# Fixed SBUF homes, a tile of its own for the first relu, and weight chunks fetched two ahead, in a fused attention, mixing and gating kernel

## The chip, the cores and the metric

The kernel runs on one core of a Trainium2 chip. The metric is the device time of one execution in microseconds (us); lower is better. A core has a matrix engine (TensorE, PE in the rows, its weight loads PEld), a vector engine (VectorE, DVE), a scalar engine (ScalarE, ACT), GpSimd (POOL) and SyncE (SP), whose queue issues the transfers of this kernel. Operands lie in SBUF, 128 partitions wide; products are collected in eight PSUM banks.

## The reference

Batch 8, 8 heads, sequence 576, head width 64, 32 memory slots; model width 512, inner width 1024.

```python
a = softmax(phi, axis=seq)                       # over the 576 positions
k_m, v_m = a^T k, a^T v                          # 32 slots per head
x = softmax(q k_m^T / 8) v_m                     # heads side by side: 576 x 512
x_prev = x shifted by one position, zero first
xk = mu_k * x + (1 - mu_k) * x_prev ;  xr likewise with mu_r
x2 = sigmoid(xr @ w_r) * (relu(xk @ w_k)**2 @ w_v)
h = relu(x2 @ w_in) ;  u, v = halves of h
v_n = (v - mean) / sqrt(var + 1e-6)
out = (u * (w_spatial @ v_n + b_spatial)) @ w_out
```

The weights arrive as 64-bit floats.

## The kernel before, in words

**Products.** To keep precision, every operand is split into a high and a low part by `split` (L124 to L128: a copy on ScalarE, a subtraction on VectorE), and a product is three matmuls: high by high, low by high, high by low. `gemm` (L102) issues them, so nearly all matmuls of the kernel have line 106; those of the wide value product have line 847. Each matmul has its own weight load of 128 columns. The moving operand has 288 columns (early and in the spatial product), 504 (the wide blocks), 256 or 512 (the last two products).

**Stages.** (1) Two attention steps and the first mixing, at 0 to about 150 us; `k_phase`, `r_phase` and `v_product` work on 288 columns twice, i = 0 and 1. (2) Eight wide blocks j = 0 to 7 of 504 columns, to about 616 us: in each, eight products K, eight V and four R in the order K0 K1 K2 V0 K3 V1 ... V5 R0 R1 R2 V6 R3 V7. K ends in a relu, a square and a split (L829, L830, `split`) into one of three slots of the tiles kh and kl, which V reads; R ends in a sigmoid (L837) out of bank 4 or 5 into tile r. (3) The products with w_in (seven products in place of eight, on 256 columns, `uv`), layer norm and the spatial product (`spatial`, 288 columns), to about 920 us. (4) The product with w_out (`project`).

**What runs between the products.** `pump()` is called 40 times in a wide block, in the middle of a product and behind it. Each call advances `att`, the generator of the attention steps 2 to 15 (`att_step`, 19 steps each), by `pace[1]`, 0.95, steps, and the generator `more[0]` by one. The end of an attention step splits its probabilities into the tile asp (ScalarE L382, VectorE L383) and, one step on, multiplies them on TensorE. The attention of block j + 2 waits until block j has made its xr. In block 6, behind K3, `more[0]` becomes `w_in_steps()`, which turns the chunks of w_in, and then of w_out, from 64-bit into 32-bit floats and forms their combinations and splits.

**Weight conversion.** `load_f64` (L155 to L180) first issues the transfer of a chunk into one of the buffers st0 and st1 (L151, SyncE's queue), and right behind it the conversion: L163 on ScalarE, L171 and L173 on VectorE. Each engine takes its instructions in order. The order itself is not quite that of the program: a planner that knows the dependences and estimates durations places an instruction earlier where it sees its operands ready; `tc.issue_after` (the `behind` of L137) forbids it to place an instruction ahead of a named one.

**Where buffers lie.** Every name has one place in SBUF; places are given out in the order in which names are first claimed, each rounded up to 32 bytes. A new tile of a name waits for the accesses to the old one. From sizes and order, the starts modulo 128 bytes are, before: kh, asp, r, t2, xs1 to xs7, AT, W1, W2, W3, st0, st1, xT1 at 0; kl, xT0, xs0, t1 at 32; t0 at 64. Inside a tile of 504 columns the low part begins 2016 bytes behind the high part, which is 96 modulo 128.

Of the kernel before, what the change touches and what calls it, by code (L numbers as in the profile page):

```python
# [38 lines left out]
WIDTHS = [1024, 1024, 1024, 1024, 512]  # L39


PARTS_K = [(0, 1, "st0"), (1, 1, "st1"), (2, 2, "xT1"), (4, 2, "kl"), (6, 1, "st0"), (7, 1, "st1")]
# [6 lines left out]
def kernel(  # L49
# [31 lines left out]
    def turns(*tags):  # L81

        while True:
            yield from tags

    ident_sb = tile_of("ident", [128, 128])
# [163 lines left out]
    def att_step(i):  # L250
# [83 lines left out]
        for halves in ((0,), (1,)) if i < 2 else ((0, 1),):  # L334
# [43 lines left out]
            else:  # L378
                for pr in range(2):
# [61 lines left out]
    def prep_x(which, c, p0, p1, both=None):  # L441
# [18 lines left out]
        if both is None:  # L460
            both = operand(n)
        h, lo = both[:, 0:p1 - p0], both[:, p1 - p0:2 * (p1 - p0)]
        split(x32, h, lo)
# [9 lines left out]
            tile_of("ATh", [128, 4096]), q0, rest[:, 0:2 * S], rest[:, 2 * S:2 * S + 256],  # L473
            rest[:, 2 * S + 256:], tile_of("asp", [128, 1792], F32R),
        ),
# [85 lines left out]
    def w_in_steps():  # L561
# [22 lines left out]
        while not att_free:  # L584
            yield
        room = tile_of("asp", [128, 1792])
        parts_of("AT", wi_v)
        for j in range(2):
            at = []
            for half in range(2):  # L590
                at.append(load_f64(part(1, half, j)))
                yield
            (a11, a12), (a21, a22) = ((v[:, 0:2], v[:, 2:4]) for v in at)
            h, lo = (p[:, :, :, 128 * j:128 * j + 128] for p in wi_v)
            raw = room[:, 0:768].rearrange("p (q c f) -> p q c f", q=3, c=2)
            add(raw[:, 0], a21, a22, ALU.add)
            add(raw[:, 1], raw[:, 0], a11)
            add(raw[:, 2], a11, a21)
            for q, a in ((0, a11), (1, a12), (2, a22), (3, raw[:, 0]), (4, raw[:, 1]), (5, raw[:, 2])):
                split(a, h[:, q], lo[:, q])  # L600
                if q % 2:
                    yield
            add(raw[:, 0], a12, raw[:, 1])
            split(raw[:, 0], h[:, 6], lo[:, 6])
            yield
        a11, a12, a21, a22 = (quads[:, half, 2 * k:2 * k + 2] for half in range(2) for k in range(2))
        s1, s2, s4 = (room[:, 512 * n:512 * n + 512].rearrange("p (c f) -> p c f", c=2) for n in range(3))
# [10 lines left out]
        for f0 in range(0, DM, 128):  # L618
            load_f64(chunks[:, :, 2 * f0:2 * f0 + 256], raw=wo_raw[:, :, f0:f0 + 128])
            yield  # L620
        for k in range(2):
# [12 lines left out]
    x2s = {}  # L634
    w1_free, xT_free, att_free = [], [], []
    copied, added, left_v, normal = [None], [None], [], []
# [83 lines left out]
    def k_phase(i, after):  # L720
        xk = [xs[0, c] for c in range(KC)]
        kh, kl = pair("k", [128, FC, HB])
        room = tile_of("r", [128, 6, HB])
        r, ks = room[:, 0:KC], room[:, KC:]
        for m in range(FC):
# [5 lines left out]
            ))  # L731
            nc.scalar.activation(out=ks[:, m % 2, :], in_=acc, func=ACTF.Relu)
            if m % 2 == 1:
                two = slice(m - 1, m + 1)
                x = ks
                nc.scalar.activation(out=x, in_=x, func=ACTF.Square)
                copied[0] = split(x, kh[:, two, :], kl[:, two, :])
# [82 lines left out]
    for j in range(NB):  # L820
        p0 = S + WB * j
        p1 = p0 + WB
        v_accs = []

# [34 lines left out]
        for n, (f, c) in enumerate(order):  # L859
            f(c)  # L860
            if f is K and c < KC:
                prep_x(1, c, p0, p1, last_xr if c == KC - 1 else None)
                if c == KC - 1:
                    mixed.add(j)
                    if j == NB - 2:
                        for _ in att:
                            pass
                        att_free.append(True)
                        more[0] = w_in_steps()
                    elif j == NB - 1:  # L870
# [344 lines left out]

    for tag, n in (("asp", 6), ("t2", 1), ("r", 7), ("xs7", 2)):
        big = tile_of(tag, [128, n * HB], F32R)
# [145 lines left out]
```

## Time and profile before

| | us |
|---|---|
| median of 3 runs | 1010.55 (1009.86 to 1014.23) |
| the profiled execution's own time | 1009.7 |
| its span | 1007.9 |
| TensorE busy | 977.4 (97%) |
| VectorE busy | 692.2 |
| ScalarE busy | 616.8 |
| GpSimd busy | 94.1 |

Matmuls overlap in TensorE's pipeline: a matmul of 504 columns is listed with about 0.39 us, but starts follow each other every 0.23 us. So a busy TensorE is not an unhindered one, and the pace is read from the distance of starts.

### The profile page before, as it was taken

The page shows a single profiled execution, that of the slowest core. Times are in us where ns is not written, and L with a number is a line of the kernel's source. Part 1 is how long each engine was busy: PE and PEld are TensorE (multiplying, and loading weights), DVE is VectorE, ACT ScalarE, POOL GpSimd, SP SyncE. Part 2 cuts the span into 40 slices and gives each one's busy share as a digit, 9 for nine tenths or more (in the row PEclk, how much of TensorE's full clock was granted, in tenths as well). Part 3 has the DMA queues.
Part 4 walks back from the last instruction along what each step waited for, and adds up shares of the span by engine and source line. Part 5 has one row for each costly group of instructions (what it writes and reads, how often), then busy time and mean ns, then how long its engine had stood idle before and what let it go on. Part 6 is the DMA issues. An engine that isn't in the chain of part 4 may idle for free.

```text
span 1007.9 us, 16735 instructions
## 1 busy us (share of the span) xinstructions
PE 977.4 (97%) x6404; PEld 855.3 (85%) x6404; DVE 692.2 (69%) x1409; ACT 616.8 (61%) x1177; POOL 94.1 (9%) x70
## 2 busy tenths in 40 slices
PE   5879999999999999999998999999999999999998
PEld 4678878787777787777887889999999999998887
DVE  4988785736757467574666417868777767869983
ACT  3786975757757577575666545936544644564653
POOL 0000000000000000000013002022012402203320
PEclk8989999999999999999999999999999999999999
DMA  9486351421334223340041502231142223155643
GB/s 279 143 259 188 114 152 64 143 79 45 122 102 143 78 56 112 102 131 1 1 154 54 169 11 84 78 113 33 58 131 86 79 78 89 56 180 162 209 147 115
DMA packets 85008, 110.93 MB, mean 110 GB/s; under 512 B 18112, under 2 KB 68416, under 8 KB 82624
## 3 DMA queue, kind: packets, MB, share of 16 engines
q1 hardware_dynamic: 84928, 109.87, 34.5%
q8 instruction: 50, 0.82, 0.3%
q14 instruction: 30, 0.25, 0.1%
HBM read 79.43 MB, written 30.41 MB: 109 GB/s over the span
## 4 chain that ended last, share of the span: by engine, by line
PE 73%; DVE 11%; ACT 11%; DMA 3%; issue 1%; POOL 1%; SPq 0%; DVEq 0%; ACTq 0%; POOLq 0%
PE bank L106 58%; PE bank L847 13%; DVE t L454 2%; DVE xs L126 1%; PE bank L289 1%; ACT t L451 1%; DMA st<-in_w_in 1%; DMA ATh<-in_kv 1%; DVE kh L126 1%; DVE r L882 1%; DVE kl L126 1%; ACT t L830 1%; ACT t L829 1%; ACT xs L125 1%; ACT L362 1%
## 5 line engine op out<-in xcount | busy, mean ns | idle before, releaser
L106 PE MATMUL bank<-xs,W1h 128*128 128x504 f32 (+2 forms) x1112 | 240.8, 335 | 0.3 <-ACT xT L943 0.3
L106 PEld LDWEIGHTS bank<-xs,W1h 128*128 128x128 f32 x1112 | 182.0, 190 | 23.2 <-issue 3.1
L847 PE MATMUL bank<-kh,W3h 128*128 128x504 f32 x384 | 129.1, 393 | 0.0
L106 PE MATMUL bank<-xs,W1l 128*128 128x504 f32 (+2 forms) x556 | 128.3, 335 | 0.0
L106 PEld LDWEIGHTS bank<-xs,W1l 128*128 128x128 f32 x556 | 94.1, 190 | 10.5 <-issue 0.2
L847 PEld LDWEIGHTS bank<-kh,W3h 128*128 128x128 f32 x384 | 72.2, 188 | 17.9 <-issue 2.8
L106 PE MATMUL bank<-xs,W2h 128*128 128x504 f32 (+3 forms) x316 | 79.8, 371 | 2.9 <-ACT r L837 2.5
L454 DVE SCALAR_TENSOR_TENSOR t<-xT,mu,t 128x288 f32<-128x288 f32 (+6 forms) x128 | 63.0, 512 | 27.1 <-ACT t L451 26.6
L106 PE MATMUL bank<-ATh,xs 128*128 128x256 f32 x472 | 75.3, 281 | 0.0
L847 PE MATMUL bank<-kh,W3l 128*128 128x504 f32 x192 | 75.1, 391 | 0.0
L829 ACT ACTIVATE t<-bank 128x504 f32<-128x504 f32 x64 | 37.5, 586 | 60.2 <-PE bank L106 52.0
L451 ACT ACTIVATE t<-xT,mu 128x288 f32<-128x288 f32 (+6 forms) x128 | 65.0, 532 | 15.0 <-DVE xs L126 14.3
L126 DVE TENSOR_TENSOR kh<-t,kh 128x504 fp32r<-128x504 f32 x48 | 33.2, 692 | 49.4 <-ACT kh L125 49.2
L106 PEld LDWEIGHTS bank<-xs,W2h 128*128 128x128 f32 x316 | 54.7, 188 | 13.6 <-ACT r L837 3.0
L106 PEld LDWEIGHTS bank<-ATh,xs 128*128 128x128 f32 x472 | 64.4, 188 | 0.1
L126 DVE TENSOR_TENSOR xs<-st,xs 128x512 fp32r<-128x512 f32 (+1 forms) x60 | 52.8, 891 | 13.7 <-ACT xs L125 13.7
L126 DVE TENSOR_TENSOR xs<-t,xs 128x504 fp32r<-128x504 f32 (+1 forms) x72 | 44.4, 624 | 24.3 <-ACT xs L125 24.0
L125 ACT ACTIVATE xs<-st 128x512 fp32r<-128x512 f32 (+1 forms) x60 | 36.1, 624 | 38.4 <-POOL st L662 35.4
L125 ACT ACTIVATE xs<-t 128x504 fp32r<-128x504 f32 (+1 forms) x72 | 39.6, 577 | 26.4 <-PE bank L106 16.2
L662 POOL TENSOR_TENSOR st<-st 128x512 f32<-128x512 f32 x16 | 23.7, 1481 | 257.3 <-DVE xs L126 256.7
L106 PE MATMUL bank<-ATl,xs 128*128 128x256 f32 x236 | 47.2, 282 | 0.0
L391 POOL MEMSET xT<- 128x4 f32 x8 | 0.9, 107 | 445.0 <-DVE t L454 366.4
(283 smaller groups left out, 2159.2 us busy)
## 6 DMA issues: line engine op xcount, KB each, us to landing
ATh<-in_kv SPq DMA_DIRECT2D x14, 1300.0 KB, 6.3
ATl<-in_qT SPq DMA_DIRECT2D x30, 288.0 KB, 4.3
st<-x2d SPq DMA_DIRECT2D x32, 256.0 KB, 3.9
ATh<-in_phin SPq DMA_DIRECT2D x15, 320.0 KB, 2.9
st<-in_w_in SPq DMA_DIRECT2D x8, 512.0 KB, 4.0
ATh<-gd SPq DMA_DIRECT2D x8, 512.0 KB, 4.9
out_T<-W3h SPq DMA_DIRECT2D x16, 256.0 KB, 2.7
out_T<-W3l SPq DMA_DIRECT2D x16, 256.0 KB, 2.6
```

The costliest lines, as they stand in the source:

```text
L106: x = nc.tensor.matmul(out=out, lhsT=pairs[i][0], rhs=pairs[i][1], start=fresh and i == 0, stop=i == n - 1, skip_group_check=not fresh,)
L125: high = nc.scalar.activation(out=h, in_=x, func=ACTF.Copy)
L126: low = nc.vector.tensor_tensor(out=lo, in0=x, in1=h.bitcast(F32), op=ALU.subtract)
L289: x = nc.tensor.matmul(out=kvp[32 * j:32 * j + 32, :], lhsT=ph[0:n, t, 32 * j:32 * j + 32], rhs=kv[0:n, t, j, :], start=(t == 0), stop=(t ...
L362: nc.scalar.activation(out=st[:, bl], in_=st[:, bl], func=ACTF.Exp, scale=scale)
L451: nc.scalar.activation(out=x, in_=xT[b][:, c, s0:s0 + w], func=ACTF.Copy, scale=mu_sb[:, 2 * KC + n:2 * KC + n + 1])
L454: nc.vector.scalar_tensor_tensor(out=x, in0=xT[b][:, c, 1 + s0:1 + s0 + w], scalar=mu_sb[:, n:n + 1], in1=x, op0=ALU.mult, op1=ALU.add,)
L662: engine.tensor_tensor(out=out, in0=a, in1=b, op=ALU.subtract)
L829: nc.scalar.activation(out=x, in_=acc, func=ACTF.Relu)
L830: nc.scalar.activation(out=x, in_=x, func=ACTF.Square)
L847: nc.tensor.matmul(out=v_accs[m], lhsT=a, rhs=b, start=c == 0 and n == 0, stop=c == FC - 1 and n == 2,)
L882: added[0] = nc.vector.tensor_tensor(out=x2, in0=v_accs[m], in1=x2, op=ALU.mult)
```

## The change

Three parts. **Homes:** all names are claimed at the start in a written order and size (`HOMES`), with a gap of 64 bytes ahead of the weights. Modulo 128, kh, kl, asp, r, t2 and xs0 to xs7 then start at 0, and W1, W2, W3, AT, st0, st1 and xT1 at 64 (xT0 at 96); the low part of a 504-column operand begins 2048 bytes behind the high part. asp becomes smaller, t2 larger. **Relu:** in `k_phase` the result of the relu goes to a new tile of t2 for each pair of m, no longer to the end of tile r. **Conversions:** `conversions()` fetches two chunks ahead of the one that it converts, with two steps on either side of each conversion; conversions and splits are placed behind the last K or R copy (`copied[0]`); `w_in_steps` starts at the head of block 6 and not behind K3, takes the AT part first and the part in xT0 second; block 7 advances it six more times. Beside these, an attention step has one more empty step between splitting its probabilities and multiplying them (20 in all), and `pace[1]` is 1.0.

```diff
+HOMES = [
+    ("ident", 512), ("mask", 32), ("mu", 64), ("eps", 32),
+    ("kh", 9216), ("kl", 9216), ("asp", 6656), ("r", 8064), ("t2", 2304),
+    ("xs0", 4096), ...
+    ("xs7", 2304), ("gap", 64),
+    ("W1h", 16384), ("W1l", 16384), ("W2h", 8192), ("W2l", 8192), ("W3h", 16384), ("W3l", 16384),
+    ("ATl", 16384), ("ATh", 16384), ("st0", 4096), ("st1", 4096), ("xT1", 9248), ("xT0", 9248),
+    ("t0", 2016), ("t1", 2016),
+]
+    for tag, n in HOMES:
+        tile_of(tag, [128, n // 4])
...
             yield True
+            if not wide:
+                yield False
...
-        h, lo = both[:, 0:p1 - p0], both[:, p1 - p0:2 * (p1 - p0)]
+        low = HB if n == 7 and p1 - p0 == HB else 512
+        h, lo = both[:, 0:p1 - p0], both[:, low:low + p1 - p0]
...
-        quads = tile_of("xT0", [128, 2, KC, HALF])
-        for half in range(2):
-            for j in range(2):
-                load_f64(part(0, half, j), raw=quads[:, half, :, 128 * j:128 * j + 128])
-                yield
-                yield
+        def conversions(todo):
+            bufs = [fetch(src) for src, _ in todo[:2]]
+            for n, (src, raw) in enumerate(todo):
+                for _ in range(2):
+                    yield
+                with behind(copied[0]):
+                    load_f64(bufs[n], raw=raw)
+                for _ in range(2):
+                    yield
+                if n + 2 < len(todo):
+                    bufs.append(fetch(todo[n + 2][0]))
...
         for j in range(2):
+            bufs = [fetch(part(1, half, j)) for half in range(2)]
+            for _ in range(4):
+                yield
             at = []
-            for half in range(2):
-                at.append(load_f64(part(1, half, j)))
+            for buf in bufs:
+                with behind(copied[0]):
+                    at.append(load_f64(buf))
                 yield
...
+        while not xT_free:
+            yield
+        quads = tile_of("xT0", [128, 2, KC, HALF])
+        yield from conversions([...])
...
-        while not xT_free:
+        while len(xT_free) < 2:
             yield
...
-            nc.scalar.activation(out=ks[:, m % 2, :], in_=acc, func=ACTF.Relu)
+            if m % 2 == 0:
+                x = tile_of("t2", [128, 2, HB])
+            nc.scalar.activation(out=x[:, m % 2, :], in_=acc, func=ACTF.Relu)
...
-    pace[:] = 0.0, 0.95
-    rings = [tile_of(tag, [128, 4, WB], F32R) for tag in ("kh", "kl")]
-    slots = [rings[0][:, 0:2], rings[0][:, 2:4], rings[1][:, 0:2]]
+    pace[:] = 0.0, 1.0
+    rings = [tile_of(tag, [128, 4, 512], F32R) for tag in ("kh", "kl")]
+    slots = [rings[0][:, 0:2, 0:WB], rings[0][:, 2:4, 0:WB], rings[1][:, 0:2, 0:WB]]
...
+        if j == NB - 2:
+            for _ in att:
+                pass
+            more[0] = w_in_steps()
...
             if j == NB - 1:
+                if 6 < n < 13:
+                    next(more[0], None)
```

## Rows read from the trace of the kernel before

**Rows 1.** The page: busy time by engine, and the granted clock in tenths.
```profile
PE 977.4 (97%) x6404; PEld 855.3 (85%) x6404; DVE 692.2 (69%) x1409; ACT 616.8 (61%) x1177; POOL 94.1 (9%) x70
...
PEclk8989999999999999999999999999999999999999
```
**Rows 2.** Stretches: stretch, sum of lengths, then busy us (instructions) per engine, granted clock, DMA.
```profile
0.00:50.00 50.00, 35.94 (x288) 29.61 (x288) 33.16 (x75) 27.69 (x49) 0.31 (x5) 0.90 0.73 213
...
500.00:550.00 50.00, 47.68 (x210) 38.92 (x208) 36.22 (x60) 34.15 (x66) 12.46 (x12) 1.00 0.33 105
...
700.00:750.00 50.00, 50.00 (x404) 49.81 (x403) 37.14 (x93) 25.98 (x56) 7.09 (x5) 1.00 0.35 109
```
**Rows 3.** What TensorE waited for over the span: us in total, times, longest.
```profile
PE bank L106 <- DVE asp L383: 3.8, 7, 0.8
PE bank L106 <- ACT r L837: 2.5, 1, 2.5
```
**Rows 4.** TensorE in block 2, 268 to 273 us: start, length, operation, count.
```profile
268.95 1.08 PE L106 MATMUL bank<-xs,W1h 128*128 128x504 f32 x4
270.49 0.77 PE L106 MATMUL bank<-asp 128*128 128x288 f32 x4 [0.46 <-DVE asp L383]
```
**Rows 5.** VectorE in the same stretch.
```profile
268.05 0.78 DVE L375 STREAM_TRANSPOSE ATl<-ATl 128x576 f32<-128x576 f32 x1
...
269.59 1.54 DVE L383 TENSOR_TENSOR asp<-ATl,asp 64x576 fp32r<-64x576 f32 x2
```
**Rows 6.** The chain of waits, 500 to 565 us: start, length, what.
```profile
516.86 4.53 DMA st<-in_w_in
...
536.34 4.45 DMA st<-in_w_out
...
548.36 1.32 ACT t L451 x2
549.68 0.48 ACT r L837
...
550.21 3.03 PE bank L106 x12
```
**Rows 7.** What ScalarE waited for, 505 to 560 us.
```profile
ACT st L163 <- DMA st<-in_w_in: 3.5, 3, 1.8
ACT st L163 <- DMA st<-in_w_out: 2.9, 2, 2.1
```
**Rows 8.** The chain of waits in block 7: V0, V1, V2 and V4, twelve matmuls each.
```profile
569.65 2.74 PE bank L847 x12
...
575.11 2.72 PE bank L847 x12
...
580.58 2.73 PE bank L847 x12
...
591.55 2.72 PE bank L847 x12
```
**Rows 9.** TensorE, u products of 256 columns, 893 to 897 us.
```profile
893.89 0.39 PE L106 MATMUL bank<-xs,W1l 128*128 128x256 f32 x2
...
894.59 0.40 PE L106 MATMUL bank<-xs,W1l 128*128 128x256 f32 x2
...
896.02 0.40 PE L106 MATMUL bank<-xs,W1l 128*128 128x256 f32 x2
...
896.74 0.40 PE L106 MATMUL bank<-xs,W1l 128*128 128x256 f32 x2
```
**Rows 10.** ScalarE ahead of the second `k_phase`'s first relu.
```profile
95.30 0.41 ACT L732 ACTIVATE r<-bank 128x288 f32<-128x288 f32 x1 [2.48 <-DMA ATh<-in_phiT]
95.75 1.39 ACT L382 ACTIVATE asp<-ATl 64x576 fp32r<-64x576 f32 x2
```
**Rows 11.** ScalarE, first and last of the splits of W1 in block 7.
```profile
598.86 1.14 ACT L125 ACTIVATE W1h<-xT 128x512 fp32r<-128x512 f32 x2
...
609.03 0.62 ACT L125 ACTIVATE W1h<-xT 128x512 fp32r<-128x512 f32 x1
```

More of the change, by code (lines that the diff above doesn't have):

```diff
@@ L39 @@
 WIDTHS = [1024, 1024, 1024, 1024, 512]
+HOMES = [
+    ("ident", 512), ("mask", 32), ("mu", 64), ("eps", 32),
+    ("kh", 9216), ("kl", 9216), ("asp", 6656), ("r", 8064), ("t2", 2304),
+    ("xs0", 4096), ("xs1", 4096), ("xs2", 4096), ("xs3", 4096), ("xs4", 4096), ("xs5", 4096), ("xs6", 4096),
+    ("xs7", 2304), ("gap", 64),
[3 more added lines that the diff above has]
+]
 PARTS_K = [(0, 1, "st0"), (1, 1, "st1"), (2, 2, "xT1"), (4, 2, "kl"), (6, 1, "st0"), (7, 1, "st1")]
@@ L473 @@
             tile_of("ATh", [128, 4096]), q0, rest[:, 0:2 * S], rest[:, 2 * S:2 * S + 256],
-            rest[:, 2 * S + 256:], tile_of("asp", [128, 1792], F32R),
+            rest[:, 2 * S + 256:], tile_of("asp", [128, 1664], F32R),
         ),
@@ L576, in part @@
             return chunks[:, :, 2 * f0:2 * f0 + 256]
-        quads = tile_of("xT0", [128, 2, KC, HALF])
-        for half in range(2):
-            for j in range(2):
-                load_f64(part(0, half, j), raw=quads[:, half, :, 128 * j:128 * j + 128])
-                yield
-                yield
-        while not att_free:
-            yield
-        room = tile_of("asp", [128, 1792])
+        def conversions(todo):
[9 more added lines that the diff above has]
+                    bufs.append(fetch(todo[n + 2][0]))
+        room = tile_of("asp", [128, 1664])
         parts_of("AT", wi_v)
         for j in range(2):
+            bufs = [fetch(part(1, half, j)) for half in range(2)]
+            for _ in range(4):
+                yield
             at = []
-            for half in range(2):
-                at.append(load_f64(part(1, half, j)))
+            for buf in bufs:
+                with behind(copied[0]):
+                    at.append(load_f64(buf))
                 yield
@@ L599, in w_in_steps @@
             for q, a in ((0, a11), (1, a12), (2, a22), (3, raw[:, 0]), (4, raw[:, 1]), (5, raw[:, 2])):
-                split(a, h[:, q], lo[:, q])
+                with behind(copied[0]):
+                    split(a, h[:, q], lo[:, q])
                 if q % 2:
@@ L603, in w_in_steps @@
             add(raw[:, 0], a12, raw[:, 1])
-            split(raw[:, 0], h[:, 6], lo[:, 6])
             yield
+            with behind(copied[0]):
+                split(raw[:, 0], h[:, 6], lo[:, 6])
+            yield
+        while not xT_free:
+            yield
+        quads = tile_of("xT0", [128, 2, KC, HALF])
+        yield from conversions([
+            (part(0, half, j), quads[:, half, :, 128 * j:128 * j + 128]) for half in range(2) for j in range(2)
+        ])
         a11, a12, a21, a22 = (quads[:, half, 2 * k:2 * k + 2] for half in range(2) for k in range(2))
@@ L617, in w_in_steps @@
         wo_raw = tile_of("xT1", [128, KC, DM])
-        for f0 in range(0, DM, 128):
-            load_f64(chunks[:, :, 2 * f0:2 * f0 + 256], raw=wo_raw[:, :, f0:f0 + 128])
-            yield
+        yield from conversions([
+            (chunks[:, :, 2 * f0:2 * f0 + 256], wo_raw[:, :, f0:f0 + 128]) for f0 in range(0, DM, 128)
+        ])
         for k in range(2):
@@ L634 @@
     x2s = {}
-    w1_free, xT_free, att_free = [], [], []
+    w1_free, xT_free = [], []
     copied, added, left_v, normal = [None], [None], [], []
@@ L722, in k_phase @@
         kh, kl = pair("k", [128, FC, HB])
-        room = tile_of("r", [128, 6, HB])
-        r, ks = room[:, 0:KC], room[:, KC:]
+        r = tile_of("r", [128, KC, HB])
         for m in range(FC):
@@ L864 @@
                     mixed.add(j)
[L865 to L870, printed above, removed]
+                    if j >= NB - 2:
                         xT_free.append(True)
@@ L1213, in chain @@
             yield from g
-    for tag, n in (("asp", 6), ("t2", 1), ("r", 7), ("xs7", 2)):
+    for tag, n in (("asp", 5), ("t2", 2), ("r", 7), ("xs7", 2)):
         big = tile_of(tag, [128, n * HB], F32R)
```

1 line of the change is left out of this document (removed).

## The prediction

> **What bounds the kernel now.** I read the page first: TensorE is busy 97% of the span and runs at its full granted clock, 2.4 GHz, after the first stage [rows 1]. By stretches, 14 of the first 50 us and about 2 us between 500 and 550 us are idle; the stretch of the narrow products has none [rows 2]. So there are two things to win: starts of matmuls that wait for another engine, and the distance between starts that wait for nothing. For the first I read TensorE's waits. Two of them can meet this change: seven waits for the split of the probabilities (VectorE L383), 3.8 us together, and one of 2.5 us for a sigmoid (L837) [rows 3]. For the second I divided start distances: twelve wide value matmuls take 2.74 us, 228 ns each [rows 8], where 504 columns at 2.4 GHz are 210 ns; six narrow ones take 0.72 us, 120 ns each [rows 9], where 256 columns are 107. These 18 and 13 ns on each of some 5200 matmuls are all that a move of buffers could touch.
>
> The listed idle understates a wait. In block 2, four starts at 228 ns from 268.95 would put the next at 269.86; it came at 270.49 [rows 4]. That is 0.63 us lost, with 0.46 listed, since the row counts only from the modelled end of the last matmul: 0.17 more for each wait. The seven cost 3.8 + 7 x 0.17 = 5.0 us, the sigmoid's 2.7.
>
> **The empty step before the attention product, and pace 1.0.** The step issues a transpose of 0.78 us, splits on ScalarE, and two subtractions of 1.54 us that end at 271.13 [rows 5]; the product behind it came too early by the 0.63 us above. One more empty step puts half a product between, six matmuls or 1.37 us [rows 8]. That covers it, and nothing else is waiting for the product: the mixing that reads it comes later in the block. It holds where each call of the pump makes one step: blocks 2 to 5 and the end of the second `k_phase` round, five of the seven. In the two earliest steps the pump makes three at once; there an extra step can fall inside a call and do nothing. Those two are at most 0.8 + 0.17 each [rows 3], 1.9 together, and stay. Gain 5.0 - 1.9 = 3.1 us; bounds 0 and 5.0. Pace 1.0 with 20 steps gives two attention steps in 40 calls, as 0.95 with 19 did, so the order repeats as before. What is late next is the K product's own eviction, which had no wait.
>
> **Conversions two ahead.** In block 6 the chain runs through transfers of weights, over 4 us each, one after the other, and at 548.36 through mixing and the sigmoid to TensorE at 550.21 [rows 6]. A conversion is issued right behind its own transfer, so ScalarE stands at L163 until it lands: five waits, 3.5 + 2.9 us [rows 7], and every relu and sigmoid queued behind it is as late. With a chunk fetched two ahead and two steps (2.7 us) and more before its use, a transfer of about 4 us has landed by then. The number of transfers (eight chunks of w_in, four of w_out), conversions and splits does not change. They start at the head of block 6, some 10 calls earlier. On SyncE's queue they stand behind block 5's stores, as they do in the program before; a fetch that waits for its buffer can hold only stores of block 6, which nobody reads before the next product. ScalarE and VectorE have room: 34 and 36 of 50 us busy there [rows 2]. The placement behind the last K copy adds no wait on ScalarE, where that copy is earlier in the same queue; on VectorE K's subtraction goes first. I count the calls: 22 for the AT part, 16 for xT0, 2 for sums, so 40 in block 6, which has 40; then 17 in block 7 from K3 on, where the six extra advances give just 17 before R0. I take 2.5 of the 2.7 us as gained; bounds 0 and 2.7. Against it I set 1.0 us for new waits (bounds 0 and 5, as many as attention's waits cost now), since block 7 now also carries the leftovers.
>
> **Relu in its own tile.** Ahead of the first relu of the second round ScalarE idles 2.48 us, shown as a transfer [rows 10]; this is the store of the last round's result out of tile r. But the attention split behind it started at 95.75 because VectorE's transpose ended at about that time, and TensorE has four banks for K. I take 0; bounds 0 and -1.0, the wait that follows it.
>
> **Homes.** Before, most pairs of moving operand and next weights lie 0 apart modulo 128. The trace has pairs 64 apart already: V1 and V4 read slot 1, whose high part begins at 64, with W3 at 0, in eight of their twelve matmuls. They take 2.72 us; V0, its high part at distance 0, takes 2.74 and V2 2.73 [rows 8]. So 64 apart gives at most 0.02 / 12 = 1.7 ns of 228, hardly over the 0.01 that the rows can tell. Among the narrow products xs0 begins at 32, so it lies 96 from W1: from 893.89 six matmuls, four of them on xs0, take 0.70 us or 117 ns; six others from 896.02 take 0.72 or 120 [rows 9]. So the narrow ones do feel the distance, by 3.3 ns at 96; no row shows them at 64. Counts from the code: 1920 of 504 and 336 of 512 columns, 1596 of 256, 1376 of 288. I take 0.5 ns on the 2256 wide ones, 1.1 us, and 1.5 ns (half of what 96 shows) on the 1596, 2.4 us, nothing on the 288: 3.5 us gained. Bounds: all that lies above the columns' own time, 18 ns x 2256 + 12 ns x 2972 = 76 us, on one side; on the other, 64 being as bad as 96 is good, a loss of 3.3 x 1596 = 5.3 us. Rows 8 are the only ones at 64, so I stay near nothing.
>
> One rule speaks against this part. The Trainium skill, page "TensorE: Matmul & The Clock Gate", Part 2: What happens when you issue a matmul, says that the moving operand and the weight load have read ports of their own, so that loading the next weights takes nothing from the running matmul. By that rule homes are worth nothing; the wide rows above agree within 0.02 of 2.74 us, the narrow ones (117 against 120 ns) do not. The same page's section Back-to-back issue gap gives columns / 2.4 plus 2.5 ns for a warm matmul by itself, for 256 columns 109 ns; an estimate from it for the most that homes could bring there is 11 ns x 1596 = 17.6 us, and no row here shows that pace.
>
> **Sum.** -3.1 - 2.5 + 1.0 - 3.5 = -8.1 us on the profiled execution's own 1009.7 (its span of 1007.9 and 1.8 around it): 1001.6. The median of the runs is 0.85 above that execution, so the median after would be 1002.4. The forecast's own range is 998 to 1007. A measurement of this kernel can tell about 0.5%, that is 1005.5 and 1015.6.
>
> **Rivals.**
> First: 64 apart is far better than any distance that the narrow products show now. Between 700 and 750 us 404 matmuls start, 124 ns each [rows 2], for 268.8 columns on average (168 of 256 and 112 of 288 per batch), 112 ns at 2.4 GHz. If half of these 12 ns goes on all 2972 narrow ones, that is 17.5 us. Then 1009.7 - 4.6 - 17.5 - 1.1 + 0.85 = 987.4. For it: xs0 shows that distance counts. Against it: slot 1. Chance 0.18.
> Second: distance counts for nothing, and xs0's 3 ns have another cause. Then the waits alone are gained, 4.6 us: 1006.0. Chance 0.15.
> Third: the change does not do what it says, because the planner moves instructions: the sigmoid's wait reappears at another R and the attention's waits shrink by half only. Then about -1.5 us: 1009. Chance 0.09.
> Fourth, slower: the splits of W1. Now they run from 598.86 to 609.7 [rows 11], in R of block 7; the u products want them about 5 us after the block's end at 616, so they have some 11 us to spare. They may start only when the last w_out chunk is converted, for which the calls just suffice. If `copied[0]` or a late buffer makes conversions miss R, seven splits at 0.6 us on ScalarE and the same on VectorE, among the splits of x2, run behind the block's end; TensorE then waits for 8 us or more and waits again between them. With the other waits gained and nothing from homes, 1009.7 + 8 - 4.6 + 0.85 = 1014, and over 1016 where the x2 splits queue up too. It decides from a slip of 11 us. Chance 0.10.
>
> **Range and chances.** The forecast has 0.48. The range 986 to 1009 holds the forecast, the second rival and half of the first and third, about 0.8. Faster by over 0.5%: the forecast but for 0.03, the first, and a little of the second, 0.66. Within 0.5%: the rest of these, the third, and a part of the fourth, 0.27. Slower: 0.07.
>
> **What would show it.** Right: the waits for L383 drop to two or three; the wait for L837 in block 6 is gone, with L163 waiting for no transfer; V's twelve matmuls stay at 2.71 to 2.74 us in all slots; six narrow ones take 0.70 to 0.72 us everywhere. The homes term is wrong if the twelve fall under 2.70, the six under 0.69, or either rises over 2.76 and 0.73. The conversions are wrong if W1's splits end after 615 us or a sigmoid is waited for again.

## The result, and the profile after

| | before | after |
|---|---|---|
| median, us | 1010.2 (1008.08 to 1014.23, 4 runs) | 1000.44 (998.18 to 1001.77, 4 runs) |
| the profiled execution's own time, us | 1009.7 | 1001.76 |
| its span, us | 1007.9 | 1000.0 |

After to before, the ratio is 0.9896, with an interval of 0.9858 to 0.9935. Taken again in another session (e9_full below) it was 0.9914 (0.9889 to 0.994). So the change brings 8.7 to 10.5 us by the two ratios, where 8.1 were forecast. Line numbers shift: `gemm` is L119, V's product L884, the first relu L766, `split` L138 and L139, the sigmoids L783 and L874, the end of an attention step L395 and L396, the conversion L176.

The page of the kernel after, against [rows 1]: TensorE's busy time and its granted clock.

```profile
PE 974.7 (97%) x6404; PEld 850.0 (85%) x6404; DVE 690.1 (69%) x1409; ACT 611.9 (61%) x1175; POOL 94.0 (9%) x70
...
PEclk9989999999999999999999999999999999999999
```

TensorE is as busy as before, 97% of a shorter span. The stretches of [rows 2] (columns as there):

```profile
0.00:50.00 50.00, 36.92 (x312) 30.70 (x312) 35.35 (x80) 30.28 (x56) 0.31 (x5) 0.97 0.79 218
500.00:550.00 50.00, 48.83 (x213) 39.75 (x213) 29.31 (x52) 32.16 (x61) 8.16 (x10) 1.00 0.29 90
700.00:750.00 50.00, 49.81 (x412) 49.58 (x411) 36.17 (x96) 28.33 (x63) 6.21 (x4) 1.00 0.28 85
```

24 more matmuls start in the first stretch, 3 more in the second and 8 more in the third. The first number is the surprise. Only a part of it is the first K product's earlier start (25.91 us behind the first matmul in place of 28.24, which hangs on the first transfers); the forecast had nothing for the rest. What TensorE waits for after, over the span (us in total, times, longest), against [rows 3]:

```profile
PE bank L287 <- DVE ATl L284: 2.4, 1, 2.4
PE bank L119 <- DVE asp L396: 1.8, 3, 0.8
...
PE bank L119 <- ACT r L874: 1.2, 1, 1.2
PE bank L119 <- ACT W3h L138: 1.0, 6, 0.2
...
PE bank L119 <- ACT xT L417: 0.2, 1, 0.2
```

Of the seven waits for the split of the probabilities three are left, with 1.8 us. The sigmoid's wait is 1.2 in place of 2.5. The first row and the fourth are new, and so is the last one in the wide blocks.

To see where the time went I took the starts of the same matmuls out of the traces, and from them the length of each stage (us; one profiled execution each):

| stage | before | after | e9_full |
|---|---|---|---|
| first matmul to first K product | 28.24 | 25.91 | 26.88 |
| to the first K of the second round | 57.12 | 43.03 | 44.11 |
| to block 0 | 41.72 | 51.47 | 51.47 |
| block 0 | 63.05 | 64.16 | 64.20 |
| blocks 1 to 5 | 309.36 | 309.24 | 309.21 |
| block 6 | 57.57 | 56.39 | 55.03 |
| block 7 | 54.74 | 54.95 | 54.94 |
| eight narrow batches | 284.08 | 282.31 | 282.17 |
| end of the spatial product, `project` | 104.30 | 104.55 | 104.52 |

From the first K product to block 0 the change takes 94.49 us where before took 98.84, 4.35 less. Of these 0.8 or so only move: 16 matmuls and a transpose of an attention step that ran in this stretch before run in block 0 after. The rest is spread: 1.2 to 2.5 in block 6, 1.8 in the narrow batches. The first line is the wait for the first transfers; over the thirteen traces of the kernel and its variants it lies between 23.8 and 28.2 us, with and without each part. Without it the stages give 5.8 us between before and after, and 6.3 to e9_full. The ratios say 10.5 and 8.7, with intervals that reach down to 6.6 and 6.1; where the rest lies, these single executions do not show.

**The first relu.** TensorE before, 47 to 58 us (start, length, operation, count, idle before and its releaser):

```profile
48.96 0.69 PE L106 MATMUL bank<-xs,W1h 128*128 128x288 f32 x4
54.51 1.82 PE L106 MATMUL bank<-asp 128*128 128x288 f32 x6 [4.85 <-ACT asp L125]
...
58.78 1.16 PE L106 MATMUL bank<-xs,W1h 128*128 128x288 f32 x4
```

and ScalarE before, in the same stretch:

```profile
56.07 0.43 ACT L125 ACTIVATE W3l<-r 128x288 fp32r<-128x288 f32 x1
...
57.32 0.70 ACT L732 ACTIVATE r<-bank 128x288 f32<-128x288 f32 x2
```

Four K products had filled their four banks by 49.7. The relu that would empty them writes to the end of a new tile r, and the old tile r is in use by attention step 1 until its split has read it, on ScalarE from 56.07 and on VectorE last:

```profile
56.60 0.45 DVE L126 TENSOR_TENSOR W3l<-r,W3l 128x288 fp32r<-128x288 f32 x1
```

That ends at 57.05, and the relu starts at 57.32. The releaser in TensorE's row (the split of asp) is only what let another product go first. ScalarE after, where the relu writes to t2:

```profile
43.24 0.41 ACT L766 ACTIVATE t<-bank 128x288 f32<-128x288 f32 x1
...
54.78 0.43 ACT L138 ACTIVATE W3l<-r 128x288 fp32r<-128x288 f32 x1
```

The relu runs 14 us earlier, and 11.5 us ahead of ScalarE's part of the split that it used to wait for. TensorE after, 58 to 68 us, shows what is late next:

```profile
58.89 0.70 PE L119 MATMUL bank<-xs,W2h 128*128 128x288 f32 x4
61.99 0.45 PE L287 MATMUL bank<-ident,ATl 128*128 128x128 f32 x1 [2.41 <-DVE ATl L284]
...
62.99 1.17 PE L119 MATMUL bank<-xs,W2h 128*128 128x288 f32 x4
```

The transpose of the next attention step waits 2.41 us for VectorE, and the products behind it wait with it. After these two holes TensorE is slow: four matmuls of 288 columns take 1.16 and 1.17 us, against 0.69 and 0.70 ahead of them. The stretches 40 to 60 and 60 to 80 us of the kernel after (columns as in [rows 2]) show where that now lies:

```profile
40.00:60.00 20.00, 17.99 (x127) 16.97 (x126) 19.48 (x43) 19.29 (x41) 0.00 (x0) 1.00 0.59 189
60.00:80.00 20.00, 17.57 (x135) 16.53 (x136) 15.49 (x27) 17.57 (x33) 0.10 (x1) 0.83 0.86 245
```

The granted clock is 1.00 and then 0.83, where before it was 0.77 and then 0.98, and 127 matmuls start in the first of the two stretches in place of 78.

In the second round, which [rows 10] showed, the tile acts as well. ScalarE after, the round's first relu and the attention split:

```profile
79.92 0.42 ACT L766 ACTIVATE t<-bank 128x288 f32<-128x288 f32 x1
...
95.62 1.39 ACT L395 ACTIVATE asp<-ATl 64x576 fp32r<-64x576 f32 x2
```

The attention split keeps its time, 95.62 in place of 95.75. The relu runs at 79.92 in place of 95.30: it no longer waits for the store out of tile r, and the K products of this round start at 73.33, between the V products of the first, where before they started behind them, at 89.60.

**Blocks 2 to 5.** TensorE after, block 2, against [rows 4]:

```profile
264.75 0.69 PE L119 MATMUL bank<-asp 128*128 128x288 f32 x4
...
266.65 1.04 PE L119 MATMUL bank<-asp 128*128 128x288 f32 x4
267.53 0.39 PE L884 MATMUL bank<-kh,W3h 128*128 128x504 f32 x1
```

The product runs in two halves of four matmuls. The first, at 264.75, no longer waits. The second takes 1.04 us, where before it took 0.68:

```profile
272.46 0.68 PE L106 MATMUL bank<-asp 128*128 128x288 f32 x4
```

Its third matmul waits until ScalarE has emptied a bank that the first half filled, which ends at 267.10:

```profile
266.71 0.39 ACT L417 ACTIVATE xT<-bank 128x288 f32<-128x288 f32 x1
```

From 266.65 to 267.53 is 0.88; four free starts of 0.132 are 0.53. So 0.35 of the 0.63 us came back inside the product.

**Blocks 6 and 7.** The chain of waits (start, length, what), against [rows 6, 8]:

```profile
527.26 0.81 POOL asp L588
528.08 6.46 DMA st<-in_w_in
...
536.07 3.29 DMA st<-in_w_in
...
542.90 0.58 ACT r L874
543.52 3.02 PE bank L119 x12
546.54 2.74 PE bank L884 x12
...
568.51 2.75 PE bank L884 x12
```

and ScalarE's wait for transfers from 495 to 625 us, against [rows 7]:

```profile
ACT st L176 <- DMA st<-in_w_in: 3.8, 1, 3.8
```

Five waits became one. Its transfer starts at 528.08, when GpSimd has read the buffer, and takes 6.46 us. Behind its conversion comes one more transfer (536.07), and behind that, as before, mixing and the sigmoid. V's twelve matmuls are 2.74 and 2.75 us, where [rows 8] had 2.72 to 2.74. The last split of W1, against [rows 11]:

```profile
602.53 0.62 ACT L138 ACTIVATE W1h<-xT 128x512 fp32r<-128x512 f32 x1
```

It starts 6.5 us earlier than before. So does the end of block 7: the split lies 7.0 us ahead of it in both kernels.

**Narrow products.** TensorE, u products (moving operand xs, weights W1), 885 to 887 us, against [rows 9]:

```profile
885.29 0.39 PE L119 MATMUL bank<-xs,W1l 128*128 128x256 f32 x2
...
885.97 0.39 PE L119 MATMUL bank<-xs,W1l 128*128 128x256 f32 x2
```

Six starts take 0.68 us, 113 ns each, where [rows 9] had 117 and 120.

### The profile page after: what moved, and what is told of

The parts are those of the page before. It is cut to its first block, busy times and chain, and to the rows that moved or that the text cites. A ratio compares the mean times of both kernels' runs of the same rounds, so it can differ in the third digit from the quotient of the medians.

```text
span 1000.0 us, 16736 instructions
## 1 busy us (share of the span) xinstructions
PE 974.7 (97%) x6404; PEld 850.0 (85%) x6404; DVE 690.1 (69%) x1409; ACT 611.9 (61%) x1175; POOL 94.0 (9%) x70
## 4 chain that ended last, share of the span: by engine, by line
PE 72%; DVE 13%; ACT 10%; DMA 2%; issue 1%; SPq 0%; POOL 0%; DVEq 0%; ACTq 0%; POOLq 0%
PE bank L119 56%; PE bank L884 14%; PE bank L302 1%; DVE xs L139 1%; DVE t L469 1%; DMA ATh<-in_kv 1%; ACT W2h L954 1%; DVE W3l L139 1%; DMA st<-in_w_in 1%; ACT W3h L138 1%; ACT t L466 1%; DVE xT L982 1%; ACT xT L417 1%; PE bank L354 1%; DVE kl L139 1%
## 5 line engine op out<-in xcount | busy, mean ns | idle before, releaser
L119 PE MATMUL bank<-xs,W1h 128*128 128x504 f32 (+2 forms) x1112 | 239.4, 333 | 1.5 <-ACT xs L138 0.6
L119 PEld LDWEIGHTS bank<-xs,W1h 128*128 128x128 f32 x1112 | 179.9, 188 | 24.9 <-issue 1.7
L119 PE MATMUL bank<-xs,W1l 128*128 128x504 f32 (+2 forms) x556 | 129.9, 335 | 0.0
L884 PE MATMUL bank<-kh,W3h 128*128 128x504 f32 x384 | 128.9, 394 | 0.0
L119 PEld LDWEIGHTS bank<-xs,W1l 128*128 128x128 f32 x556 | 92.0, 188 | 14.9 <-issue 5.1
L884 PEld LDWEIGHTS bank<-kh,W3h 128*128 128x128 f32 x384 | 72.3, 188 | 15.4
L119 PE MATMUL bank<-xs,W2h 128*128 128x504 f32 (+3 forms) x316 | 81.5, 377 | 1.2 <-ACT r L874 1.2
L884 PE MATMUL bank<-kh,W3l 128*128 128x504 f32 x192 | 75.4, 393 | 0.0
L119 PE MATMUL bank<-ATh,xs 128*128 128x256 f32 x472 | 74.6, 279 | 0.0
L119 PEld LDWEIGHTS bank<-xs,W2h 128*128 128x128 f32 x316 | 56.3, 195 | 12.0 <-issue 1.7
L119 PEld LDWEIGHTS bank<-ATh,xs 128*128 128x128 f32 x472 | 64.1, 188 | 0.2
L139 DVE TENSOR_TENSOR kh<-t,kh 128x504 fp32r<-128x504 f32 x48 | 32.7, 681 | 42.3 <-ACT kh L138 42.2
L139 DVE TENSOR_TENSOR xs<-st,xs 128x512 fp32r<-128x512 f32 (+1 forms) x60 | 51.6, 870 | 13.7 <-ACT xs L138 13.6
L138 ACT ACTIVATE xs<-t 128x504 fp32r<-128x504 f32 (+1 forms) x72 | 40.4, 578 | 32.9 <-PE bank L119 24.8
L139 DVE TENSOR_TENSOR xs<-t,xs 128x504 fp32r<-128x504 f32 (+1 forms) x72 | 45.4, 641 | 20.3 <-ACT xs L138 20.0
L138 ACT ACTIVATE xs<-st 128x512 fp32r<-128x512 f32 (+1 forms) x60 | 36.1, 623 | 36.9 <-POOL st L695 34.0
L119 PE MATMUL bank<-ATl,xs 128*128 128x256 f32 x236 | 46.8, 280 | 0.0
L884 PE MATMUL bank<-kl,W3h 128*128 128x504 f32 x128 | 42.4, 392 | 0.0
```

What stands on the lines that cost most here:

```text
L119: x = nc.tensor.matmul(out=out, lhsT=pairs[i][0], rhs=pairs[i][1], start=fresh and i == 0, stop=i == n - 1, skip_group_check=not fresh,)
L138: high = nc.scalar.activation(out=h, in_=x, func=ACTF.Copy)
L139: low = nc.vector.tensor_tensor(out=lo, in0=x, in1=h.bitcast(F32), op=ALU.subtract)
L884: nc.tensor.matmul(out=v_accs[m], lhsT=a, rhs=b, start=c == 0 and n == 0, stop=c == FC - 1 and n == 2,)
```

## Experiments

The ratios are to the kernel before, from runs of the same session, with their intervals; the differences between two ratios carry an uncertainty, the root of the sum of the squares of the two half intervals. There were three sessions: one with e1 to e4, one with e5 and e7 to e9, one with e6 and e10 to e12. Where e6, e10 or e11 is set against e9_full, the two ratios come from different sessions.

**Each part alone.** Four kernels, each the one before with one part of the change.

e1_relu (asp is 512 bytes smaller, as in the change, to make room):
```diff
-        room = tile_of("r", [128, 6, HB])
-        r, ks = room[:, 0:KC], room[:, KC:]
+        r = tile_of("r", [128, KC, HB])
...
+            if m % 2 == 0:
+                x = tile_of("t2", [128, 2, HB])
+            nc.scalar.activation(out=x[:, m % 2, :], in_=acc, func=ACTF.Relu)
```


> Kernel before with the relu part alone: the first relu's result goes to a tile of t2; asp is cut to 6656 bytes to make room, which leaves every start modulo 128 as it was. Theory A (the lead at block 0, 6.7 us in the changed kernel, comes from the first relu no longer waiting until attention step 1 has let go of tile r): 5 to 7 us faster than before, the first relu at about 43 us instead of 57, TensorE's wait of 4.85 us at 54 us gone. Theory B (as I predicted: the tile is worth 0 to 1 us, and the lead comes from homes or from the attention's order): within 1 us of before.

Measured: 1007.39 against 1009.79 us, ratio 0.9972 (0.9953 to 0.9991), 2.8 us. The part that I had priced at nothing is worth something by itself. Its trace has no wait of 4.85 us at the first relu; first K to block 0 is 96.52 us against 98.84. It has two new waits there (TensorE's waits, 0 to 110 us):

```profile
PE bank L106 <- DVE asp L383: 2.6, 1, 2.6
PE bank L274 <- DVE ATl L271: 2.4, 1, 2.4
```

The second stays in the whole change, as the list of its waits shows. The first does not: there no wait for the split of the probabilities is over 0.8 us. Which part takes it away is not shown; it is just as small in the kernel after without the empty step (e10_no_step, 0.8) and without homes (e6_no_homes, 0.9).

e2_homes:
```diff
+    for tag, n in HOMES:
+        tile_of(tag, [128, n // 4])
...
-        h, lo = both[:, 0:p1 - p0], both[:, p1 - p0:2 * (p1 - p0)]
+        low = HB if n == 7 and p1 - p0 == HB else 512
+        h, lo = both[:, 0:p1 - p0], both[:, low:low + p1 - p0]
```


> Kernel before with the homes alone (addresses, low parts 2048 bytes behind the high ones), order of work as before. Theory A (narrow products on 256 columns 2 to 3 ns faster, wide ones on 504 columns 1 ns slower, 288 unchanged): 1596 x 2.5 = 4 us gained, 1920 x 1 = 2 us lost, so 1 to 3 us faster; the twelve value matmuls 2.75 us, block 0 reached no earlier than before. Theory B (homes bring the lead at block 0): 6 us faster and the lead there at block 0. Theory C (ports of their own): no change at all, twelve 2.73 us and six 0.71 to 0.72.

Measured: 1009.32, ratio 0.9996 (0.998 to 1.0013). Nothing that the times can tell. But the starts did change: the mean distance, those over 1.1 times the median left out as waits, is 116.1 ns at 256 columns (before 118.8) and 228.9 at 504 (before 228.2). Times the counts, 2.7 x 1596 = 4.3 us are gained and 0.7 x 1920 = 1.3 lost; and a wait for the split of the spatial weights (W3h), 0.7 us in four, is new in the narrow batches.

e3_conv (the new `conversions`, the start at the head of block 6, the six advances in block 7):
```diff
+                with behind(copied[0]):
+                    load_f64(bufs[n], raw=raw)
...
+                if n + 2 < len(todo):
+                    bufs.append(fetch(todo[n + 2][0]))
...
+            more[0] = w_in_steps()
```


> Kernel before with the conversions alone (two chunks fetched ahead, placed behind the last K copy, started at the head of block 6). Theory A (they take the sigmoid's wait of 2.5 us in part): the way from block 6 to block 7 falls from 57.6 to 55.5 to 56.5 us, in all 1 to 2 us faster. Theory B (they only shift ScalarE's lateness): block 6 stays at 57 us or more, no change.

Measured: 1005.17, ratio 0.9967 (0.9951 to 0.9984), 3.3 us. Block 6 is 55.53 us against 57.57. TensorE's only wait from 495 to 625 us:

```profile
PE bank L106 <- ACT r L858: 0.5, 1, 0.5
```

e4_step:
```diff
+            if not wide:
+                yield False
...
-    pace[:] = 0.0, 0.95
+    pace[:] = 0.0, 1.0
```


> Kernel before with the empty step and pace 1.0 alone. Theory A (the product waits for VectorE's split in blocks 2 to 5 and ahead of block 0, as predicted): four waits of 0.6 us and one of 1.0 gone, 3 us faster, blocks 2 to 5 at 61.9 us instead of 62.5. Theory B (the wait is taken over by another one or the order ahead of block 0 gets worse): blocks 2 to 5 at 62.4 us or more, less than 1 us gained.

Measured: 1009.18, ratio 0.999 (0.9975 to 1.0006), 1.0 us and not told from none. TensorE's waits from 130 to 495 us, where before has five for L383 with 2.3 us:

```profile
PE bank L106 <- DVE asp L383: 0.7, 1, 0.7
PE bank L106 <- ACT xT L404: 0.5, 3, 0.2
```

The old wait is gone four times out of five, and three times another took its place: the second half of the product waits until ScalarE has emptied a bank of the first. Blocks 2, 3 and 4 by the starts: 62.29, 62.37 and 62.21 us against 62.57, 62.55 and 62.41, 0.66 together, where three waits of 0.63 would be 1.9.

The four alone sum to 2.8 + 0.4 + 3.3 + 1.0 = 7.5 us, the whole brings 8.7 to 10.5. The difference is within the intervals.

**One part taken out of the whole.** e9_full is the change again, as their measure.

> The changed kernel itself, timed again beside the three others. If the parts simply add (relu 2.8, homes 0.4, conversions 3.3, step 1.0 by their single ratios, 7.5 together), 0.9925 of before; if they help each other, 0.990 or less, as first measured.

Measured: 1001.09 against 1008.46, ratio 0.9914 (0.9889 to 0.994). Block 6 is 55.03 us with no wait for a sigmoid, so the 1.2 in the change's first profile is not in every execution.

e7_no_relu (the reverse of e1_relu's edit, in the kernel after):
```diff
-            if m % 2 == 0:
-                x = tile_of("t2", [128, 2, HB])
-            nc.scalar.activation(out=x[:, m % 2, :], in_=acc, func=ACTF.Relu)
+            nc.scalar.activation(out=ks[:, m % 2, :], in_=acc, func=ACTF.Relu)
```


> Changed kernel with the relu part undone: the first relu goes to the end of tile r again. Theory A (the relu is the larger part of the lead at block 0): 3 to 5 us slower than the changed kernel, TensorE waiting 4 to 5 us at about 54 us, block 0 as late as in the kernel before. Theory B (the lead has other sources): within 1 us of the changed kernel.

Measured: 1005.55, ratio 0.9961 (0.9945 to 0.9977): the relu's own tile is worth 0.0047, 4.7 us with an uncertainty of 3.0. The old wait is back in TensorE's timeline:

```profile
51.33 1.82 PE L119 MATMUL bank<-asp 128*128 128x288 f32 x6 [4.81 <-ACT asp L138]
```

By the starts, first K to block 0 is 98.38 us, as before the change (98.84), and 94.49 and 95.58 with it. In and out of the other parts, this tile alone decides that wait. The stage says the same over the thirteen traces: first K to block 0 is 93.8 to 96.5 us in the eight kernels with the tile and 98.4 to 103.4 in the five without. Whether the tile is worth more among the other parts (4.7) than alone (2.8) the uncertainties do not tell.

e6_no_homes (the kernel after, without `HOMES` and with low parts 2016 bytes behind):
```diff
-    for tag, n in HOMES:
-        tile_of(tag, [128, n // 4])
...
-    rings = [tile_of(tag, [128, 4, 512], F32R) for tag in ("kh", "kl")]
+    rings = [tile_of(tag, [128, 4, WB], F32R) for tag in ("kh", "kl")]
```


> Changed kernel without the homes: buffers lie as before modulo 128, low parts 2016 bytes behind; asp and t2 are sized as in the change to make room. Theory A (homes bring 2 ns on 256 columns and cost 0.7 ns on 504): 256 columns 118.8 ns, 504 columns 228.2, a wide block 0.2 us shorter, a batch of the narrow stage 0.2 us longer, in all 0 to 1.5 us slower than the changed kernel, 0.992 to 0.993 of before. Theory B (homes matter more with the other parts in place): 3 us or more slower, 0.9945 or more.

Measured: 1002.41 against 1008.37, ratio 0.9923 (0.9901 to 0.9945). Against e9_full homes are worth 0.0009, 0.9 us with an uncertainty of 3.4. By the starts of the two traces (after and this one) homes make the eight narrow batches 2.0 us shorter and blocks 0 to 5 and 7 together 0.6 longer.

e5_gap0 (all homes kept, the 64 bytes ahead of the weights gone, so that operands and weights both start at 0):
```diff
-    ("xs7", 2304), ("gap", 64),
+    ("xs7", 2304), 
```


> Changed kernel without the gap of 64 bytes: the same order of claims and the low parts 2048 bytes behind, but operands and weights 0 apart modulo 128. Theory A (the distance decides the pace: 256 columns 118.8 to 119 ns at 0 against 116.1 at 64, 504 columns 228 at 0 against 228.9 at 64, 288 equal): narrow stage 2.0 us longer per the eight batches (34.97 us each instead of 34.77), a wide block 0.2 us shorter, in all 0 to 2 us slower than the changed kernel. Theory B (the order of the buffers does it, not the distance): 116 ns and 229 ns stay.

Measured: 1004.78, ratio 0.9956 (0.9937 to 0.9976), 0.0042 or 4.2 us (uncertainty 3.2) slower than the change. TensorE, u products of 256 columns, 752 to 755 us:

```profile
752.19 0.64 PE L119 MATMUL bank<-xs,W1h 128*128 128x256 f32 x4
...
752.91 0.64 PE L119 MATMUL bank<-xs,W1h 128*128 128x256 f32 x4
```

Six starts take 0.72 us, 120 ns each; a narrow batch takes 35.22 us, against 34.77 with the gap and 34.97 before. So the gap does act, and eight batches of 0.45 us would account for 3.6 of the 4.2. Over the kernel before it gains less. There not all lay at 0: xs0 lay at 32, and its products had 117 ns in [rows 9].

e10_no_step (the reverse of e4_step's edit, in the kernel after):
```diff
-            if not wide:
-                yield False
...
-    pace[:] = 0.0, 1.0
+    pace[:] = 0.0, 0.95
```


> Changed kernel without the empty step, pace 0.95 as before. Theory A (the step gives what its blocks show, 0.2 to 0.3 us each, because the second half of the attention product then waits for the first half's eviction): blocks 2 to 5 longer by 0.2 to 0.4 us each, 1 to 2 us slower than the changed kernel, about 0.993. Theory B (the step is worth the 0.63 us that each wait cost): 3 us slower, 0.9945.

Measured: 1001.67, ratio 0.9941 (0.9924 to 0.9957). Against e9_full the step is worth 0.0027, 2.7 us with an uncertainty of 3.0. By the starts blocks 2, 3 and 4 are 62.68, 62.65 and 62.51 us against 62.37, 62.47 and 62.27 after: 0.73. Both agree with 1; what lies between 0.7 and 2.7 is open.

**Can the new wait be won too?** e8_late places the transpose of attention step 2 behind the last matmul of the V product, so that nothing stands behind its wait:
```diff
+        with behind(*([last_v[0]] if i == 2 else [])):
+            x = nc.tensor.transpose(out=bc, in_=mx.to_broadcast([128, 128]), identity=ident_sb)
...
+        last_v[0] = gemm(acc, prods, 0, 2)
```


> Changed kernel with one more order: the transpose that opens attention step 2 on TensorE is placed behind the last V matmul issued by then, not among the R products, where TensorE waited 2.4 us for it at 60 us and then ran for some 6 us at half its granted clock. Theory A (the early lead is cut by that wait and by the slow clock behind it): 2 to 5 us faster than the changed kernel. Theory B (the wait hides another one, ScalarE being as late): no gain, the wait reappears at another place before 130 us.

Measured: 1002.6, ratio 0.9938 (0.9914 to 0.9963): nothing gained. TensorE's waits, 0 to 110 us:

```profile
PE bank L119 <- ACT W3h L192: 2.8, 1, 2.8
PE bank L303 <- ACT ATh L294: 2.1, 1, 2.1
```

The wait for the transpose is gone, and V now waits for its weights on ScalarE, and the attention for its later operand. In this stretch ScalarE, not the order on TensorE, is what ends last. The slow starts behind the hole are gone too; TensorE in e8_late, and its stretch from 60 to 80 us:

```profile
63.91 0.67 PE L119 MATMUL bank<-kh,W3h 128*128 128x288 f32 x3 [2.78 <-ACT W3h L192]
64.41 0.69 PE L119 MATMUL bank<-xs,W2h 128*128 128x288 f32 x4
```

```profile
60.00:80.00 20.00, 14.50 (x136) 13.62 (x135) 18.32 (x33) 19.01 (x35) 0.00 (x0) 1.00 0.88 260
```

Four matmuls take 0.69 us behind a hole of 2.78, and the granted clock stays at 1.00. Yet first K to block 0 is 94.32 us, against 94.49 and 95.58 with the slow starts. So, as far as this run shows, the slow starts were not what the stage's length hung on.

**What the distance does.** e12_distance leaves the whole kernel out, and what it stores is a fill. It runs 48 matmuls in a row per case, with weights at 0 and the moving operand so placed that the weights lie d bytes on, modulo 128; TensorE alone, then again beside a busy ScalarE and VectorE.
```diff
+    for x in some(48, 256, (16,)):
+        nc.tensor.matmul(**x)  # 256 columns, weights 64 bytes on
```


> No part of the kernel: streams of 48 matmuls on TensorE alone (the output is a fill), each with its own weight load, for 256, 288, 504 and 512 columns and weights 0, 16, 32, 64, 96 and 112 bytes on modulo 128; then mixtures of high and low parts, and six streams beside ScalarE copies and VectorE subtractions. Theory A (moving operand and weight load meet in SBUF, and the distance decides): 256 columns about 120 ns at 0 and 116 at 64, 504 columns some 1 ns apart, the same with the other engines idle. Theory B (ports of their own; the differences come from VectorE and ScalarE): one pace per width whatever the distance, and differences only in the six streams beside busy engines.

Measured, TensorE's timeline (48 matmuls each, 256 columns at 0 and 16, then 504 at 0 and 16):

```profile
21.54 5.92 PE L50 MATMUL bank<-mv,wt 128*128 128x256 f32 x48
27.29 5.66 PE L52 MATMUL bank<-mv,wt 128*128 128x256 f32 x48
...
93.58 11.06 PE L74 MATMUL bank<-mv,wt 128*128 128x504 f32 x48
104.48 11.52 PE L76 MATMUL bank<-mv,wt 128*128 128x504 f32 x48
```

The mean distance of starts within each case, in ns:

| columns | 0 | 16 | 32 | 64 | 96 | 112 |
|---|---|---|---|---|---|---|
| 256 | 119.8 | 114.6 | 120.0 | 117.8 | 116.6 | 116.9 |
| 288 | 131.7 | 134.5 | 131.6 | 132.2 | 133.4 | 131.8 |
| 504 | 227.1 | 236.9 | 229.4 | 228.7 | 226.7 | 226.6 |
| 512 | 227.6 | 231.0 | 233.5 | 229.3 | 233.4 | 231.5 |

Each is one stream of one execution. Beside busy engines it is 119.8, 117.9 and 116.6 for 256 columns at 0, 64 and 96, and 227.1, 228.6 and 226.7 for 504: the same within 0.1 ns, so for these the place of the buffers decides and not the traffic of the others. The best distance differs from width to width: 16 is best for 256 and worst for 288 and 504, and 64 is best for none.

Of the probe's mixtures of high and low parts, two have the kernel's distance: 504 columns 64 apart, with the low part 2048 or 2016 bytes behind the high one. Both are at 228.7 ns. e11_mix, planned beside the probe, tries the second in the kernel after.
```diff
-        low = HB if n == 7 and p1 - p0 == HB else 512
-        h, lo = both[:, 0:p1 - p0], both[:, low:low + p1 - p0]
+        h, lo = both[:, 0:p1 - p0], both[:, p1 - p0:2 * (p1 - p0)]
```


> Changed kernel with the low parts of 504-column operands right behind the high ones again (2016 bytes, 96 modulo 128), homes 64 apart for all else. Theory A (it is the even distance of 64 that costs the wide products 0.7 ns, and a mixture as in the kernel before does better): 504 columns 228.2 to 228.5 ns, a wide block 0.1 to 0.2 us shorter, 1 us faster than the changed kernel, too little for the timed ratio but plain in the blocks. Theory B (64 apart for the high part alone costs as much): 228.9 ns or more, blocks unchanged.

Measured: 1000.33 against 1008.37, ratio 0.9914 (0.9897 to 0.993). By the starts, wide matmuls are 228.5 ns apart and not 228.9, and blocks 1 to 5 are 0.06 to 0.11 us shorter each than after. The probe's two streams did not show these 0.4 ns. That is too little for the times: it equals the change and does not beat it.

## Why the prediction was right, and where it was not

The time, 1002.4 forecast and 1000.44 measured, came right as a sum whose terms were partly wrong: the relu's gain was missed, those of the empty step and of homes were taken too large, and what was set against the conversions for new waits hardly came. That these errors nearly cancel is luck.

**Relu: 0 forecast, 4.7 us (uncertainty 3.0) measured within the change, 2.8 alone.** This is the step that failed most. It argued from ScalarE's wait in the second round [rows 10]: the attention split behind that relu would hold everything to its time. The split does keep its time (95.62 in place of 95.75), but the K products and the first relu do not hang on it; they start 16 and 15 us earlier, between the V products. And the step did not look at the first round, where the old tile r belongs to attention step 1. The longest of all TensorE's waits before, 4.85 us at 49.7 to 54.5 us, stood under a split of asp and was not among the two waits that the prediction took up:

```profile
PE bank L106 <- ACT asp L125: 5.7, 2, 4.9
```

That the banks of K were full, and why, is seen from ScalarE's and VectorE's order alone.

**Empty step: -3.1 forecast, about -1 measured** (-1.0 alone, -0.7 by the starts, up to -2.7 by the times within the change). That waits in the wide blocks go and two early ones stay was right: three are left with 1.8 us, one more than counted, in about the time that I had left for two (1.9). What failed is "what is late next": I named the eviction of a K product, which had no wait. The attention product is issued in two halves, and the second waits for an eviction of the first, 0.35 of the 0.63 us in block 2.

**Conversions: -2.5 and +1.0 forecast, -3.3 (interval -4.9 to -1.6) measured.** Block 6 is 1.2 to 2.7 us shorter in the traces of the change and of its variants, as the sigmoid's wait allowed. The new waits hardly came: block 7 is 0.2 us longer, and 0.01 with the conversions alone. One sign failed: ScalarE still stands for a transfer, 2.1 to 3.8 us in the nine traces with this part. In the change's first trace that transfer starts only when GpSimd has read its buffer, and then takes 6.46 us, more than the 4 that I had allowed. In five of the nine traces the slack covers it; in three 0.5 us of it reached TensorE through a sigmoid, in the change's first one 1.2. W1's splits end at 603, so the fourth rival did not come.

**Homes: -3.5 forecast, -0.4 (-2.0 to 1.3) alone and -0.9 (uncertainty 3.4) within the change.** Both terms were off in size, one in sign. The 256 columns gained 2.6 ns and not 1.5, 4.1 us on 1596 starts; the 504 lost 0.7 ns where 0.5 were to be won, 1.3 us on 1920. By the sign I set (six under 0.69 us) the term is wrong, and it is: 0.68. And TensorE, faster in the narrow batches, now waits six times for the split of the spatial weights. That is 1.0 us as listed; by the starts of the 288-column products, those that come late lose 3.3 us where they lost 1.5. So the batches give back only 1.8 us. The 288 columns, taken as untouched, lost 0.4 ns there, 0.3 us. The second rival, homes worth nothing, was nearer in this part; its time of 1006.0 lacked the relu. The first rival is out: of its 6 ns for every narrow start, 2.6 came at 256 columns and none at 288.

The rule of the Trainium skill that I set against this part (page "TensorE: Matmul & The Clock Gate", Part 2: What happens when you issue a matmul: operand and weights are read through ports of their own) does not carry as far as I took it, to one pace whatever the places. With TensorE alone and nothing but the operand's place changed, starts were 114.6 to 120.0 ns apart at 256 columns and 226.6 to 236.9 at 504. And between e5_gap0 and the change the u products keep their operand at 0 and only their weights move by 64 bytes: 120.0 ns and 113.8 (stretches of 36 starts and more). So the place of the weights counts too. Whether the two reads meet, or one of them is slower by itself, no run here shows.

**The third rival**, that the planner moves instructions, is seen twice, without harm: K products of the second round moved between V products of the first, and 16 matmuls of an attention step into block 0.

## What to carry to other kernels

When a tile is shared by two uses, look at each round in which a new one is claimed, the first above all: the row names the last releaser, and only the order on the engine that frees the banks tells which old reader held it. A wait that is covered is worth what is left until the next one on the same product, so price the second eviction before counting the first as gained. Placing buffers by a rule of bytes is worth measuring width by width; a few ns per matmul of one width can be lost again at another, and what is won goes first to the next wait.

## What the runs showed of the hardware

- The place of operand and weights moved the distance of starts by up to 5 ns of 120 (256 columns) and 10 of 227 (504) with other engines idle; the three distances that were repeated beside busy engines gave the same within 0.1 ns. The distance alone does not set it. In the kernel after, u products have the moving operand at 0 and the weights at 64 and start every 113.8 ns, in stretches of 36 and more; v products (moving operand AT at 64, weights xs at 0) every 117.8, as the probe's case with those places. With the gap gone both are at 120. At 504 columns the probe and the kernel do not agree (227.1 with all at 0, 229.5 in e5_gap0), and why is open.
- Holes of 2.41 us (after) and 4.85 (before) in TensorE's work were followed by starts of 288 columns every 0.24 us in place of 0.13, which is the lower level of its clock (1.2 and not 2.4 GHz). Not every hole was: behind 2.78 us in e8_late and behind the sigmoid's 2.53 us in block 6 of the kernel before, the granted clock stayed at 1.00. What sets the two kinds apart is open.
